# Last stage of a three-part kernel: VectorE's order written out, the weight conversions one at a time, their buffers in other places

## The chip, the cores and the metric

The kernel runs on one core of a Trainium2 chip, as one launch. The metric is the device time of one execution in microseconds (us). TensorE (PE) multiplies, VectorE (DVE), ScalarE (ACT) and GpSimd (POOL) do elementwise work, and SyncE's queue (SP) issues every DMA. Each of them takes its instructions in the order of its own list and waits at the head of that list for semaphores.

## The reference

Attention, then two two-layer networks, all in float32; only the second network matters here:

```python
def _moe2_ref(x, w_in, w_out) -> np.ndarray:
    h = x @ w_in
    relu6 = np.clip(h + 3.0, 0.0, 6.0)
    g = h * relu6 / 6.0
    return (g @ w_out).astype(np.float32)
```

There are 2304 tokens, 512 model channels and 2048 inner channels. `x` comes from the attention and the first network. The weights reach the kernel as 64-bit floats.

## The kernel before

A float32 product of full precision is built from three matmuls on rounded operands: each operand is split into a high part (`hi`, rounded by ScalarE, line 160) and a low part (`lo`, the rest, subtracted by VectorE, line 161), and hi·hi, hi·lo and lo·hi are added up in PSUM. `split` (line 158) is that pair of instructions.

The kernel runs through the attention, the first network, and then the second network in two stages. **Its first stage** (the loop at line 1008) has 32 steps. A step takes one quarter `g` of the tokens and one pair of channel blocks `j` (0 to 7) and does seven products of 6 matmuls (line 879). ScalarE holds partial sums in `z` and `m5` (line 886), VectorE adds to them (889), the gate takes one instruction of each engine (892 and 893), and the result goes to the DRAM tensor `g_scratch` (898). The products of step `j` read `w2[j]`, which lies in the buffers `wi{j}0`, `wi{j}1`, `wo{j}0` and, two steps together, `wo{j}1`. The last four steps are quarter 3 with j = 4 to 7, here called steps 28 to 31.

**Its second stage** multiplies by `w_out`. Tokens 0 to 1023 are done in two *plain blocks* of 512 tokens (`plain`, line 1042). A block takes 16 chunks `k` of 128 inner channels; a chunk has four token tiles of three matmuls of 512 columns (line 1147), 12 in all, so a block has 192. For a chunk, `gr` is loaded from `g_scratch` (1136, two chunks per load, three buffers), and split into `gh` and `gl` (three buffers each). In the second block, `make_forms` (1046) also builds from pairs of weight chunks the combinations (`tt`, then `wf2`, lines 1055 to 1063) that the remaining 1280 tokens need (line 1172, results `m`). After each block ScalarE moves the four sums to `ot` (1152), of which there are two buffers, and they are stored.

**The weights of the second stage** come in 16 chunks `k`, as 64-bit words (`wraw`, loaded by `load_out`, line 961). `to_f32` (132) turns one chunk into float32 bits: ScalarE (142), two GpSimd instructions (144, 147), two of VectorE (152, 155). The split into `wo` follows (160 on ScalarE, 161 on VectorE). `split_out` does all of it for one chunk. Chunks 0 to 7 are converted during the first stage through a spare buffer (`wcv`). Chunks 8 to 15 are called from the first plain block, one at each even `k` (line 1130), and their float32 goes to buffers `wf` that stay until `make_forms` has read them; these take the places of `w2` weights that are used no more. Which places is set by the list `slots` (950):

```python
slots = [f"{nm}{j}{i}" for j in range(4, NU) for nm in ("wi", "wo") for i in range(2)]
slots.append(slots.pop(slots.index("wo51")))
...
direct[j] = wp.tile([P, 2, CH], U32, tag=slots[NJ + j], name="wf")
```

Chunks 8 and 9 share `direct[4]`, 10 and 11 `direct[5]`, and so on; `NJ` is 8, so the four lie at slots 12 to 15: `wi71`, `wo70`, `wo71`, `wo51`.

**What sets the order.** The program is written once; a scheduler then moves instructions on each engine's list by a simulated time line, except those wrapped in `keep_in_program_order`, which keep their written order among each other. In the first plain block nothing of `split` and `to_f32` is kept; in the second, both instructions of `split(gh, gl, ...)` and VectorE's part of `make_forms` are.

Of the kernel before, what the change touches and what calls it, by code (L numbers as in the profile page):

```python
# [10 lines left out]
F32R = mybir.dt.float32r  # L11
# [4 lines left out]
P = 128  # L16
# [24 lines left out]
U32 = mybir.dt.uint32  # L41
# [20 lines left out]
def attention_moe_moe(ctx, tc, qt, kt, kq2, kqs, vs4, vp, s, w_in1, w_out1, alpha, w_in2, w_out2, out):  # L62
# [9 lines left out]
    FC = DFF // P  # L72
# [14 lines left out]
    wp = ctx.enter_context(tc.tile_pool(name="wp", bufs=1))  # L87
# [25 lines left out]
    CH = 512  # L113
# [18 lines left out]
    def to_f32(raws, pool, tag, bufs, keep, beside):  # L132

        ops = []
        for r, by in zip(raws, beside):
            c = pool.tile([P, CH], U32, tag=tag, bufs=bufs, name="wcv")
            half = r.bitcast(U16).rearrange("p f (t b) -> p f t b", t=2)
            ops.append((c, c.bitcast(F32), r[:, :, 1], r[:, :, 0], (half[:, :, 1, 0], half[:, :, 0, 1]) if by else None))

        for c, cf, high, low, by in ops:  # L140
            first = tc.keep_in_program_order if bufs == WB0 else keep
            first(nc.scalar.activation(cf, high.bitcast(F32), AF.Copy, scale=W_SCALE))  # L142
        for c, cf, high, low, by in ops:
            keep(nc.gpsimd.tensor_scalar(cf, cf, W_MOST, -W_MOST, op0=ALU.min, op1=ALU.max))  # L144

        for c, cf, high, low, by in ops:
            keep(nc.gpsimd.tensor_scalar(high.bitcast(F32), cf, 0.0, 1.0, op0=ALU.mult, op1=ALU.mult))
        for c, cf, high, low, by in ops:
            if by:
                keep(nc.scalar.activation(*by, AF.Copy, scale=1.0 / 8192, bias=-4095.5 / 8192))  # L150
        for c, cf, high, low, by in ops:
            keep(nc.vector.scalar_tensor_tensor(c, c, 3, high, op0=ALU.logical_shift_left, op1=ALU.bitwise_or))  # L152
        for c, cf, high, low, by in ops:
            if not by:
                keep(nc.vector.scalar_tensor_tensor(c, low, 29, c, op0=ALU.logical_shift_right, op1=ALU.bitwise_or))
        return [cf for c, cf, *_ in ops]

    def split(hi, lo, of, keep=lambda ins: ins):

        keep(nc.scalar.activation(hi, of, AF.Copy))  # L160
        keep(nc.vector.tensor_tensor(lo, of, hi.bitcast(F32), op=ALU.subtract))
# [589 lines left out]
    with ExitStack() as st:  # L751
        pool = Pools(st, tc, "att0", ("wcv", "vraw", "t pT"), WB0)
# [15 lines left out]
    with ExitStack() as st:  # L768
        pool = Pools(st, tc, "sb1", ("wcv g5 gh5 gl5",), WB)
        stage(s=[0], pt=[2], pv=[2], y=[1, 3, 4, 5])  # L770
        it = moe1(w1, (0, 1), pool, ("g5", "gh5", "gl5", SKEW + 1), SKEW)
        f = 0
# [34 lines left out]
    with ExitStack() as st:  # L807
        pool = Pools(st, tc, "attb", ("kraw qraw vraw ks qh vs", "t", "xf pth ptl"))
# [14 lines left out]
    NJ = FC // 2  # L823
# [28 lines left out]
    with ExitStack() as st:  # L852
        pool = Pools(st, tc, "last", ("g5 gh5 gl5 wcv",), WB)
# [94 lines left out]
    wo2, outs = {}, []  # L948
    chunks = [j + h * NJ for j in range(NJ) for h in range(2)]
    slots = [f"{nm}{j}{i}" for j in range(4, NU) for nm in ("wi", "wo") for i in range(2)]  # L950
    slots.append(slots.pop(slots.index("wo51")))
    direct = {}
# [21 lines left out]
        def tile(self, *args, **kw):  # L974
            return self.of

    def split_out(k):

        f = chunks[k]
        pool = cv  # L980
        if k >= FC // 2:
            j = f % NJ
            if j not in direct:
                direct[j] = wp.tile([P, 2, CH], U32, tag=slots[NJ + j], name="wf")
            pool = Half(direct[j][:, f // NJ])
        (cf,) = to_f32([outs[k]], pool, "wcv", 2, lambda ins: ins, (False,))
        t = wp.tile([P, 2, CH], F32R, tag=places[k][0], name="wo")
        split(t[:, 0], t[:, 1], cf)
        wo2[f] = (t[:, 0], t[:, 1])

    A1, B1 = 3, 4
    order = [(0, j) for j in range(A1)] + [(1, j) for j in range(NJ)] + [(0, j) for j in range(A1, NJ)]
# [6 lines left out]
    with ExitStack() as ph2:  # L999
# [8 lines left out]
        for i, (g, j) in enumerate(order):  # L1008
            if i in (1, 3, 5):
                with tc.high_priority(offset=WLP):  # L1010
                    w2.append(split_pair(units2[len(w2)], cv, 2))
            if i == ends[1] + 2:
                xs[2] = load_x(xb, 2)
            if i == ends[0] + 2:
                xs[3] = load_x(xa, 3)
            if i == ends[2] + 2:
                xbs.close()
                gp = late.enter_context(tc.tile_pool(name="late", bufs=2))
            if i >= ends["w", 0] + 2:
                for _ in range(2):  # L1020
                    if len(outs) < FC - 2 and i >= ends["w", places[len(outs)][1]] + 2:
                        load_out(len(outs))
                if len(wo2) < min(len(outs) - 1, FC // 2):
                    with tc.high_priority(offset=WLP):
                        split_out(len(wo2))
            step = Step(g, j, i % 2)
            if last is None:
                with tc.high_priority(offset=60):
                    for product in (step.first, step.second, step.fifth, step.sixth):
                        product()  # L1030
            else:
                for product in (step.first, last.seventh, step.second, last.third, step.sixth, step.fifth, last.fourth):
                    product()
            last = step
# [11 lines left out]
        def make_forms(j):  # L1046

            if j in direct:
                wf = direct[j].bitcast(F32)
            else:  # L1050
                wf = gp.tile([P, 2, CH], F32, tag="wf", bufs=1, name="wf")
                for h in range(2):
                    hi, lo = wo2[j + h * NJ]
                    tc.keep_in_program_order(
                        nc.vector.tensor_tensor(wf[:, h], hi.bitcast(F32), lo.bitcast(F32), op=ALU.add)
                    )
            tt = fp.tile([P, 4, ND], F32, tag="s", name="tt")
            b11, b12, b21, b22 = (wf[:, h, c * ND : (c + 1) * ND] for h in range(2) for c in range(2))
            for dst, x, y in ((0, b12, b11), (1, b22, tt[:, 0]), (2, b22, b12), (3, b21, tt[:, 1])):
                tc.keep_in_program_order(nc.vector.tensor_tensor(tt[:, dst], x, y, op=ALU.subtract))  # L1060
            t = []
            for i in range(2):
                hl = wp.tile([P, 2, 2, ND], F32R, tag=slots[2 * j + i], name="wf2")
                split(hl[:, 0], hl[:, 1], tt[:, 2 * i : 2 * i + 2])
                t += [(hl[:, 0, c], hl[:, 1, c]) for c in range(2)]
            q = [tuple(x[:, c * ND : (c + 1) * ND] for x in wo2[j + h * NJ]) for h in range(2) for c in range(2)]
            forms.append([q[0], t[2], q[2], q[3], t[0], t[1], t[3]])
# [52 lines left out]
        steps = [(t0, jp) for t0 in rest for jp in range(NJ // 2)]  # L1120
        ahead = []
        stage(o=[2, 5, 7, 0, 6, 3, 4, 1], m=[2, 5, 7, 0, 6, 3, 4, 1])
        free = lambda ins: ins
        for bi, t0 in enumerate(plain):
            ntt = NB2 // P
            op = [bank("o") for i in range(ntt)]
            for k, f in enumerate(chunks):
                if bi == 0 and k < 2:
                    load_out(len(outs))
                if bi == 0 and len(wo2) < FC and k % 2 == 0:  # L1130
                    split_out(len(wo2))
                if bi == 1 and k % 2:
                    make_forms(k // 2)
                if k % GC == 0:
                    gr = gp.tile([P, GC, NB2], F32, tag="gr", bufs=3, name="gr")
                    nc.sync.dma_start(gr, g_d.rearrange("(h j p) t -> j p h t", h=2, p=P)[f, :, :, t0 : t0 + NB2])
                gh = gp.tile([P, NB2], F32R, tag="gh", bufs=3, name="gh2")
                gl = gp.tile([P, NB2], F32R, tag="gl", bufs=3, name="gl2")
                split(gh, gl, gr[:, k % GC], tc.keep_in_program_order if bi else free)
                wh, wl = wo2[f]  # L1140
                if bi == 1 and k == FC - 4:
                    ahead.append(left_forms(*steps[0]))
                    fp.tile([P, LINE], F32, tag="line", bufs=1, name="line")
                for i in range(ntt):
                    tsl = slice(i * P, (i + 1) * P)
                    for lt, r in ((gh, wh), (gh, wl), (gl, wh)):
                        nc.tensor.matmul(  # L1147
                            op[i], lt[:, tsl], r, start=(k == 0 and r is wh and lt is gh), stop=(k == FC - 1 and lt is gl)
                        )
            for i in range(ntt):  # L1150
                ot = stg.tile([P, DM], F32, tag="yt", name="ot")
                nc.scalar.activation(ot, op[i], AF.Copy, scale=1.0 / 6.0)
                store_rows(t0 + i * P, ot)
# [61 lines left out]
```

## Time and profile before

| | us |
|---|---|
| median of three runs (1006.7, 1006.78, 1008.31) | 1006.78 |
| profiled execution, own time | 1007.25 |
| its span, first to last instruction | 1005.4 |
| PE busy | 973.0 (97%) |
| DVE busy | 696.3 (69%) |
| ACT busy | 648.3 (64%) |
| POOL busy | 449.2 (45%) |
| mean granted TensorE clock | 0.981 of full speed |

The clock is granted at full speed (1.0, 2.4 GHz) or half (0.5, 1.2 GHz); a number between is a mean over a stretch. A busy PE counts overlapping matmuls as one busy stretch, so the distance between the starts of neighbouring matmuls tells the rate. In the timeline, times are counted from the span's start.

### The profile page before, as it was taken

Reading aid. Unit: us, or ns where it says so; the run is one execution under the profiler, and the core shown is the slowest. Engines: PE = TensorE matmul, PEld = TensorE weight load, DVE = VectorE, ACT = ScalarE, POOL = GpSimd, SP = SyncE. Lnnn points to the kernel's source line nnn. Section 1 sums busy time; section 2 is a strip of 40 time slices with the busy share of each in tenths; the row PEclk is TensorE's granted clock in tenths of the full one; section 3 lists DMA queues with packets and bytes.
Section 4 is the critical chain, followed back from the end, with each engine's and each line's share of the span. In section 5 each row is a group of like instructions: output and inputs, shape, how many; then the busy total and the mean of one; then the engine's idle time right before and its main releaser. Section 6 shows DMA issues by size and latency. Waiting matters only on the chain.

```text
span 1005.4 us, 19017 instructions
## 1 busy us (share of the span) xinstructions
PE 973.0 (97%) x6578; PEld 889.9 (89%) x6578; DVE 696.3 (69%) x1655; ACT 648.3 (64%) x1442; POOL 449.2 (45%) x597
## 2 busy tenths in 40 slices
PE   7789999999999999999999999999999979999998
PEld 5568788999999998998998888999999967789998
DVE  5778884566666666666654885977658691997774
ACT  6568778678768778778754665756657652454342
POOL 5554667657666667666644763533112230000001
PEclk9779999999999999999999999999999999999999
DMA  6990014113122223122105332434258642344441
GB/s 207 303 359 3 24 30 131 40 46 91 52 76 73 59 68 97 52 70 79 52 14 185 99 104 82 166 118 147 113 189 280 238 127 84 106 146 148 126 127 42
DMA packets 64504, 114.53 MB, mean 114 GB/s; under 512 B 6280, under 2 KB 30648, under 8 KB 64408
## 3 DMA queue, kind: packets, MB, share of 16 engines
q1 hardware_dynamic: 64408, 113.32, 34.8%
q8 instruction: 52, 0.85, 0.4%
q14 instruction: 44, 0.36, 0.1%
HBM read 84.84 MB, written 28.46 MB: 113 GB/s over the span
## 4 chain that ended last, share of the span: by engine, by line
PE 88%; DVE 4%; ACT 3%; DMA 2%; issue 2%; SPq 0%; POOL 0%; ACTq 0%; DVEq 0%; POOLq 0%
PE h L248 20%; PE y L675 20%; PE m L1172 10%; PE a L879 10%; PE o L1147 7%; PE b L879 5%; PE s L410 4%; PE pv L472 4%; PE pt L447 4%; PE c L879 2%; PE pv L603 1%; PE s L322 1%; DMA wraw<-in_w_in 1%; PE pt L593 1%; DVE wf L152 1%
## 5 line engine op out<-in xcount | busy, mean ns | idle before, releaser
L248 PE MATMUL h<-xhi,wi 128*128 128x256 f32 (+1 forms) x896 | 227.6, 322 | 2.8 <-DVE gt L698 1.5
L248 PEld LDWEIGHTS h<-xhi,wi 128*128 128x128 f32 x896 | 156.7, 191 | 16.3 <-DVE gt L698 1.9
L675 PE MATMUL y<-gh,wo 128*128 128x256 f32 (+1 forms) x896 | 162.1, 315 | 0.0
L675 PEld LDWEIGHTS y<-gh,wo 128*128 128x128 f32 x896 | 133.8, 190 | 11.3 <-ACT gh L701 0.4
L248 PE MATMUL h<-xlo,wi 128*128 128x256 f32 (+1 forms) x448 | 143.4, 320 | 0.0
L879 PE MATMUL a<-x,wc 128*128 128x288 f32 x768 | 113.2, 295 | 1.1 <-ACT z L886 1.1
L879 PEld LDWEIGHTS a<-x,wc 128*128 128x128 f32 x768 | 106.0, 188 | 1.9 <-ACT z L886 1.6
L144 POOL TENSOR_SCALAR wcv<-wcv 128x512 f32<-128x512 f32 x56 | 42.0, 759 | 114.2 <-ACT wcv L142 111.2
L675 PE MATMUL y<-gl,wo 128*128 128x256 f32 (+1 forms) x448 | 91.6, 317 | 0.0
L422 POOL TENSOR_SCALAR t<-t,rec 128x384 f32<-128x384 f32 (+2 forms) x96 | 65.4, 683 | 57.5 <-DVE rec L421 32.3
L248 PEld LDWEIGHTS h<-xlo,wi 128*128 128x128 f32 x448 | 85.8, 191 | 5.9
L413 DVE CUSTOM_DVE_ANT_0 t<-s,mask 128x384 f32<-128x384 f32 (+2 forms) x96 | 53.4, 562 | 53.4 <-PE pt L447 34.1
L698 DVE SCALAR_TENSOR_TENSOR gt<-gt,beta,h 128x256 f32<-128x256 f32 (+1 forms) x112 | 61.6, 552 | 30.7 <-ACT gt L697 29.5
L1147 PE MATMUL o<-wo,gh 128*128 128x512 f32 x256 | 74.6, 406 | 7.9 <-ACT wo L160 4.2
L1112 POOL TENSOR_TENSOR ot<-u,e 128x256 f32<-128x256 f32 x5 | 3.9, 783 | 171.5 <-DVE u L1106 153.9
L418 ACT ACTIVATE t<-t,m 128x384 f32<-128x384 f32 (+2 forms) x96 | 67.1, 700 | 17.0 <-DVE m L413 15.8
L675 PEld LDWEIGHTS y<-gl,wo 128*128 128x128 f32 x448 | 69.7, 190 | 6.0 <-issue 0.2
L702 POOL TENSOR_TENSOR gl<-gt,gh 128x256 fp32r<-128x256 f32 x80 | 59.1, 740 | 30.2 <-ACT gh L701 28.3
L701 ACT ACTIVATE gh<-gt 128x256 fp32r<-128x256 f32 (+1 forms) x112 | 53.1, 477 | 29.7 <-DVE gt L698 28.1
L383 POOL TENSOR_TENSOR ks<-kraw,ks 64x576 fp32r<-64x576 f32 (+1 forms) x40 | 52.4, 1311 | 41.1 <-issue 33.6
L1147 PEld LDWEIGHTS o<-wo,gh 128*128 128x128 f32 x256 | 50.0, 197 | 20.2 <-ACT wo L160 4.7
L697 ACT ACTIVATE gt<-h 128x256 f32<-128x256 f32 (+1 forms) x112 | 48.7, 439 | 20.8 <-PE h L248 14.4
(172 smaller groups left out, 2390.2 us busy)
## 6 DMA issues: line engine op xcount, KB each, us to landing
g_scratch<-gt SPq DMA_DIRECT2D x64, 288.0 KB
wraw<-in_w_in SPq DMA_DIRECT2D x32, 512.0 KB
wraw<-in_w_out SPq DMA_DIRECT2D x32, 512.0 KB
gq<-g_scratch SPq DMA_DIRECT2D x40, 256.0 KB
kraw<-in_kt SPq DMA_DIRECT2D x32, 288.0 KB
gr<-g_scratch SPq DMA_DIRECT2D x16, 512.0 KB
qraw<-in_qt SPq DMA_DIRECT2D x32, 160.0 KB
vraw<-in_vp SPq DMA_DIRECT2D x32, 160.0 KB
```

The source lines that it names most:

```text
L248: nc.tensor.matmul(dst, lt, r, start=first and i == 0, stop=last and i == len(terms) - 1)
L383: nc.gpsimd.tensor_tensor(ks[D:P], kraw[D:P], ks[D:P].bitcast(F32), op=ALU.subtract)
L413: nc.vector.tensor_tensor_reduce(t[:n, a:e], sc[:n, : e - a], mask[:n, MASK + n - (e - a) :][:, : e - a] if e == w else mask[:n, : e - a], ...
L418: nc.scalar.activation(t[:n, :w], t[:n, :w], AF.Exp, bias=m[-1][:n], scale=-1.0, accum_out=den[:n])
L422: nc.gpsimd.tensor_scalar(t[:n, :w], t[:n, :w], rec[:n], 1.0, op0=ALU.mult, op1=ALU.mult)
L675: nc.tensor.matmul(ys[dc // per][:, o : o + n], which[:, dc * P : (dc + 1) * P], gg, start=(f == 0 and which is wl and dc % per == 0), sto ...
L698: nc.vector.scalar_tensor_tensor(gt, gt, beta[:, f : f + 1], hp[:, :n], op0=ALU.mult, op1=ALU.add)
L701: nc.scalar.activation(gh, gt, AF.Copy)
L702: (nc.vector if n == 512 else nc.gpsimd).tensor_tensor(gl, gt, gh.bitcast(F32), op=ALU.subtract)
L879: nc.tensor.matmul(dst[:, :NX2], lt, r, start=first and n == 0, stop=n == len(terms) - 1, skip_group_check=not first,)
L1147: nc.tensor.matmul(op[i], lt[:, tsl], r, start=(k == 0 and r is wh and lt is gh), stop=(k == FC - 1 and lt is gl))
L1172: nc.tensor.matmul(acc[i], lt, r, start=(j == 0 and x == 0 and k % 2 == 0), stop=(j == NJ - 1 and x == 2 and (k % 2 == 1 or k == 6)),)
```

## The change

There are four parts. The buffers of `direct` move from slots 12 to 15 to slots 0 to 3 (`wi40`, `wi41`, `wo40`, `wo41`), and those of `wf2` move four slots on. `split_out` is cut in two, `out_f32` (to float32) and `split_out` (into hi and lo), and the first plain block calls the one at odd and the other at even `k`, one chunk at a time, behind the `split` of that chunk. VectorE's instructions of these, from k = 3 on and in the whole second block, keep their written order (`in_order`); ScalarE's are left to the scheduler in both blocks. `make_forms` is called behind the `split` of its chunk.

```diff
+    def in_order(ins):
+        return tc.keep_in_program_order(ins) if ins.ins.engine == mybir.EngineType.DVE else ins
+
+    def out_f32(k, keep=free):
...
-                direct[j] = wp.tile([P, 2, CH], U32, tag=slots[NJ + j], name="wf")
+                direct[j] = wp.tile([P, 2, CH], U32, tag=slots[j - NJ // 2], name="wf")
             pool = Half(direct[j][:, f // NJ])
-        (cf,) = to_f32([outs[k]], pool, "wcv", 2, lambda ins: ins, (False,))
+        return to_f32([outs[k]], pool, "wcv", 2, keep, (False,))
+
+    def split_out(k, cf, keep=free):
+
         t = wp.tile([P, 2, CH], F32R, tag=places[k][0], name="wo")
-        split(t[:, 0], t[:, 1], cf)
-        wo2[f] = (t[:, 0], t[:, 1])
+        split(t[:, 0], t[:, 1], cf[0], keep)
+        wo2[chunks[k]] = (t[:, 0], t[:, 1])
...
-                        split_out(len(wo2))
+                        split_out(len(wo2), out_f32(len(wo2)))
...
-                hl = wp.tile([P, 2, 2, ND], F32R, tag=slots[2 * j + i], name="wf2")
+                hl = wp.tile([P, 2, 2, ND], F32R, tag=slots[(NJ // 2 + 2 * j + i) % len(slots)], name="wf2")
...
-                if bi == 0 and len(wo2) < FC and k % 2 == 0:
-                    split_out(len(wo2))
-                if bi == 1 and k % 2:
-                    make_forms(k // 2)
+                hold = in_order if bi or k > 2 else free
+                if bi == 0 and k == 0:
+                    split_out(FC // 2, out_f32(FC // 2))
...
-                split(gh, gl, gr[:, k % GC], tc.keep_in_program_order if bi else free)
+                split(gh, gl, gr[:, k % GC], hold)
+                if bi == 0 and k and k % 2 == 0:
+                    split_out(FC // 2 + k // 2, cf, hold)
+                if bi == 0 and k % 2 and k < FC - 1:
+                    cf = out_f32(FC // 2 + k // 2 + 1, hold)
+                if bi == 1 and k % 2:
+                    make_forms(k // 2)
```

All five engines' lists are unchanged up to the last steps of the first stage. Three places differ most.

VectorE's list where chunk 8 is converted. `wf_10914` is the float32 of chunks 8 and 9, `wo_10920` the split weights of chunk 8; `gl2_11098` belongs to chunk 8 of the first plain block. Before:

```order
L152 SCALAR_TENSOR_TENSOR wf_11086<-wf_11086,wraw_10603 128x512
L161 TENSOR_TENSOR gl2_11098<-gr_11095,gh2_11097 128x512
L155 SCALAR_TENSOR_TENSOR wf_11086<-wraw_10603,wf_11086 128x512
L152 SCALAR_TENSOR_TENSOR wf_10914<-wf_10914,wraw_10453 128x512
L161 TENSOR_TENSOR gl2_11114<-gr_11095,gh2_11113 128x512
L161 TENSOR_TENSOR wo_11134<-wf_11086,wo_11134 128x512
L152 SCALAR_TENSOR_TENSOR wf_10914<-wf_10914,wraw_10455 128x512
L155 SCALAR_TENSOR_TENSOR wf_10914<-wraw_10453,wf_10914 128x512
L152 SCALAR_TENSOR_TENSOR wf_11171<-wf_11171,wraw_10912 128x512
L155 SCALAR_TENSOR_TENSOR wf_10914<-wraw_10455,wf_10914 128x512
L161 TENSOR_TENSOR gl2_11140<-gr_11137,gh2_11139 128x512
```

Now, with `gl2_10986` belonging to chunk 3 of the block and `gt`, `z` and `m5` to the last steps of the first stage:

```order
L893 SCALAR_TENSOR_TENSOR gt_10765<-gt_10765,a_10687 128x288
L152 SCALAR_TENSOR_TENSOR wf_10914<-wf_10914,wraw_10453 128x512
L155 SCALAR_TENSOR_TENSOR wf_10914<-wraw_10453,wf_10914 128x512
L161 TENSOR_TENSOR wo_10920<-wf_10914,wo_10920 128x512
L889 TENSOR_TENSOR m5_8672<-a_10749,m5_8672 128x288
L889 TENSOR_TENSOR z_10812<-c_10830,z_10812 128x288
L889 TENSOR_TENSOR z_10750<-b_10794,z_10750 128x288
L893 SCALAR_TENSOR_TENSOR gt_10827<-gt_10827,m5_8672 128x288
L152 SCALAR_TENSOR_TENSOR wf_10914<-wf_10914,wraw_10455 128x512
L893 SCALAR_TENSOR_TENSOR gt_10845<-gt_10845,z_10750 128x576
L155 SCALAR_TENSOR_TENSOR wf_10914<-wraw_10455,wf_10914 128x512
L161 TENSOR_TENSOR wo_10970<-wf_10914,wo_10970 128x512
```

Chunk 8, which stood behind the conversions of chunks 10 to 13 and 15 and beside the `gl` of its own use, now stands first of the eight, ahead of the `gl` of chunk 3.

ScalarE's list at steps 28 and 29 (`gt_10703` and `z_10614` are of step 28, `z_10688` of step 29). Before:

```order
L892 ACTIVATE gt_10629<-a_10539,three_78 128x288
L886 ACTIVATE z_10688<-a_10687 128x288
L892 ACTIVATE gt_10703<-m5_8672,three_78 128x288
L892 ACTIVATE gt_10721<-z_10614,three_78 128x576
L160 ACTIVATE gh2_10925<-gr_10923 128x512
L160 ACTIVATE gh2_10943<-gr_10923 128x512
L886 ACTIVATE z_10688<-a_10687 128x288
```

Now, `wraw_10601` and `wraw_10603` being chunks 12 and 13, the last two that are loaded before the `gr`:

```order
L892 ACTIVATE gt_10629<-a_10539,three_78 128x288
L142 ACTIVATE wf_11074<-wraw_10601 128x512
L886 ACTIVATE z_10688<-a_10687 128x288
L142 ACTIVATE wf_10914<-wraw_10453 128x512
L142 ACTIVATE wf_10914<-wraw_10455 128x512
L142 ACTIVATE wf_11074<-wraw_10603 128x512
L892 ACTIVATE gt_10703<-m5_8672,three_78 128x288
L892 ACTIVATE gt_10721<-z_10614,three_78 128x576
L160 ACTIVATE gh2_10925<-gr_10923 128x512
L160 ACTIVATE gh2_10943<-gr_10923 128x512
L886 ACTIVATE z_10688<-a_10687 128x288
```

Four conversions that stood beside and behind step 31 are now between steps 28 and 29; two more (chunks 10 and 11) follow ahead of step 30's first `z`.

ScalarE's list between the two plain blocks: `gh2_11240` is chunk 15 of the first, the next two `gh2` are chunks 0 and 1 of the second. Before:

```order
L160 ACTIVATE gh2_11240<-gr_11222 128x512
L1152 ACTIVATE ot_11256<-o_10908 128x512
L1152 ACTIVATE ot_11259<-o_10909 128x512
L1152 ACTIVATE ot_11262<-o_10910 128x512
L1152 ACTIVATE ot_11265<-o_10911 128x512
L160 ACTIVATE gh2_11274<-gr_11272 128x512
```

Now:

```order
L160 ACTIVATE gh2_11240<-gr_11219 128x512
L160 ACTIVATE gh2_11274<-gr_11272 128x512
L160 ACTIVATE gh2_11290<-gr_11272 128x512
L1165 ACTIVATE ot_11256<-o_10908 128x512
L1165 ACTIVATE ot_11259<-o_10909 128x512
L160 ACTIVATE gh2_11322<-gr_11320 128x512
L160 ACTIVATE wf2_11302<-tt_11297 128x512
L160 ACTIVATE wf2_11305<-tt_11297 128x512
L1165 ACTIVATE ot_11262<-o_10910 128x512
L160 ACTIVATE gh2_11338<-gr_11320 128x512
```

The first two `gh` of the second block moved ahead of all four `ot`, and the last two `ot` behind them.

## Rows read from the trace of the kernel before

**Rows 1.** The page's first part: TensorE's busy time, share, instructions.

```profile
PE 973.0 (97%) x6578; PEld 889.9 (89%) x6578; DVE 696.3 (69%) x1655; ACT 648.3 (64%) x1442; POOL 449.2 (45%) x597
```

**Rows 2.** Windows: length, busy us per engine (instructions), granted clock, DMA share, GB/s.

```profile
786.00:795.50 9.50, 8.65 (x65) 8.42 (x64) 8.37 (x17) 7.29 (x16) 0.00 (x0) 1.00 0.75 258
...
822.50:826.70 4.20, 0.01 (x1) 0.00 (x0) 4.20 (x8) 1.78 (x3) 0.00 (x0) 1.00 0.52 163
826.70:835.00 8.30, 7.42 (x19) 5.38 (x20) 4.18 (x7) 1.89 (x3) 0.00 (x0) 0.59 0.07 20
...
855.20:860.00 4.80, 4.55 (x13) 3.37 (x14) 4.70 (x10) 2.00 (x5) 0.00 (x0) 0.68 0.24 86
860.00:900.00 40.00, 40.00 (x177) 33.13 (x178) 38.85 (x76) 19.65 (x32) 0.00 (x0) 1.00 0.38 113
```

**Rows 3.** Timeline of TensorE: start, us, instruction, [idle before, releaser].

```profile
822.12 0.39 PE L1147 MATMUL o<-wo,gl 128*128 128x512 f32 x1
826.75 1.46 PE L1147 MATMUL o<-wo,gh 128*128 128x512 f32 x4 [4.23 <-ACT wo L160]
...
851.12 0.62 PE L1147 MATMUL o<-wo,gh 128*128 128x512 f32 x2
...
851.80 0.62 PE L1147 MATMUL o<-wo,gh 128*128 128x512 f32 x2
852.25 0.39 PE L1147 MATMUL o<-wo,gl 128*128 128x512 f32 x1
855.26 3.48 PE L1147 MATMUL o<-wo,gh 128*128 128x512 f32 x8 [2.62 <-ACT gh L160]
...
859.84 2.11 PE L1147 MATMUL o<-wo,gh 128*128 128x512 f32 x8 [0.19 <-ACT gh L160]
...
900.77 0.52 PE L1172 MATMUL m<-wo,ga 128*128 128x256 f32 x3
```

**Rows 4.** Timeline of ScalarE at the two holes.

```profile
826.06 0.63 ACT L160 ACTIVATE wo<-wf 128x512 fp32r<-128x512 f32 x1 [1.86 <-DVE wf L155]
...
850.64 1.28 ACT L1152 ACTIVATE ot<-o 128x512 f32<-128x512 f32 x2 [5.71 <-PE o L1147]
853.42 1.27 ACT L1152 ACTIVATE ot<-o 128x512 f32<-128x512 f32 x2 [1.51 <-DMA out<-ot]
854.59 0.62 ACT L160 ACTIVATE gh<-gr 128x512 fp32r<-128x512 f32 x1
```

**Rows 5.** The chain of waits: the first `gr` load. Columns: start, us, what.

```profile
780.44 5.63 DMA gr<-g_scratch
```

**Rows 6.** Timeline of SyncE's queue: the loads of chunks 12 and 13.

```profile
776.75 0.94 SPq L965 DMA_DIRECT2D wraw<-in_w_out  x2
```

**Rows 7.** Timeline of ScalarE, steps 28 to 30 of the first stage.

```profile
780.65 0.49 ACT L892 ACTIVATE gt<-a,three 128x288 f32<-128x288 f32 x1
...
786.10 1.15 ACT L160 ACTIVATE gh<-gr 128x512 fp32r<-128x512 f32 x2 [1.23 <-DMA gr<-g_scratch]
787.15 0.39 ACT L886 ACTIVATE z<-a 128x288 f32<-128x288 f32 x1
...
789.35 0.40 ACT L886 ACTIVATE z<-a 128x288 f32<-128x288 f32 x1
```

**Rows 8.** Timeline of TensorE: step 29's seventh, step 30's sixth, three products up to step 30's seventh.

```profile
787.60 1.07 PE L879 MATMUL a<-x,wc 128*128 128x288 f32 x6 [0.84 <-ACT z L886]
...
790.09 0.96 PE L879 MATMUL a<-x,wc 128*128 128x288 f32 x6
...
791.68 2.56 PE L879 MATMUL a<-x,wc 128*128 128x288 f32 x18
```

**Rows 9.** Timeline of VectorE: the gate that frees a PSUM bank.

```profile
793.22 0.45 DVE L893 SCALAR_TENSOR_TENSOR gt<-gt,a 128x288 f32<-128x288 f32 x1 [0.41 <-ACT gt L892]
```

**Rows 10.** Tile `wf` from 770 to 860: count, ns min/median/max, first and last start, form.

```profile
L142 ACT ACTIVATE wf<-wraw x8: 656/669/681, 799.0 to 814.6; 128x512 f32<-128x512 f32 x8
...
L152 DVE SCALAR_TENSOR_TENSOR wf<-wf,wraw x8: 685/890/1120, 807.2 to 825.9; 128x512 uint32<-128x512 uint32 x8
```

More of the change, by code (lines that the diff above doesn't have):

```diff
@@ L975, in tile, with free @@
             return self.of
-    def split_out(k):
+    def free(ins):
+        return ins
+    def in_order(ins):
+        return tc.keep_in_program_order(ins) if ins.ins.engine == mybir.EngineType.DVE else ins
+    def out_f32(k, keep=free):
         f = chunks[k]
@@ L1122, in attention_moe_moe @@
         stage(o=[2, 5, 7, 0, 6, 3, 4, 1], m=[2, 5, 7, 0, 6, 3, 4, 1])
-        free = lambda ins: ins
         for bi, t0 in enumerate(plain):
```

## The prediction

> **What bounds the kernel now.** I read the page first: TensorE is busy 97% of the span, and no other engine over 70% [rows 1]. So only a change that shortens TensorE's idle time or its slow clock moves the end. The lists are the same up to the last steps of the first stage, at about 781 us; I read everything from there to the end of the second plain block. The windows there [rows 2] show where TensorE isn't full: a little in 786 to 795.5 (8.65 of 9.50 us), nothing in 822.5 to 826.7, a mean clock of 0.59 behind that, and 0.68 in 855.2 to 860. The mean of 0.59 is a mix of half speed (1.2 GHz) and full speed. From 860 to 900 TensorE is full at clock 1.00. So two holes, each with a stretch of half clock behind it.
>
> TensorE's own timeline gives their places [rows 3]. The first stands before the 97th matmul of the first plain block (96 have started by 822.12), that is at chunk 8: TensorE waits 4.23 us for ScalarE's `wo`. ScalarE's timeline has that instruction at 826.06, itself late because VectorE's line 155 was [rows 4]. VectorE was busy for all of 4.20 us in that window [rows 2]: it was working through conversions of later chunks, as its list shows, since chunks 8 and 9 go to `wi71`, a weight buffer of the last step, and are converted behind those of 10 to 13 and 15. The second hole stands between the blocks: 2.62 us until `gh` of the second block's chunk 0, which ScalarE does at 854.59, behind four `ot`, two of which wait for the store of the first two [rows 4]. From 860 on VectorE is busy 38.85 of 40 us [rows 2], which matters for what could go wrong.
>
> **What the two holes cost.** At full clock three matmuls start in 851.80 − 851.12 = 0.68 us, so one in 0.227 [rows 3]. Chunk 8 would have started at 822.12 + 0.23 = 822.35, and 96 matmuls later, at 844.1, the block would have been over. It was over at 852.25 + 0.23 = 852.48. First hole with its clock: 8.4 us. From 852.48 to the first `m` at 900.77 are 48.3 us; 192 matmuls need 43.5. Second hole with its clock and a wait of 0.19 [rows 3]: 4.8 us. Together 13.1 (13.2 by the rounded terms).
>
> **What the change does to them.** The new places `wi40` to `wo41` are freed by step 28, not 31. Chunk 8 becomes the first conversion on VectorE, ahead of `gl` of chunk 3, five chunks or 5 × 12 × 0.227 = 13.6 us ahead of its use; each later one is written four chunks ahead of its use, with one conversion (three instructions of VectorE, 0.69 each alone [rows 10]) and two `gl` of the same size for every two chunks: 5 × 0.69 = 3.45 us of VectorE in 5.44 us of TensorE. So I take the first hole as gone. At the second, `gh` of chunks 0 and 1 stand before the `ot`, and their buffers are free when TensorE has done chunks 13 and 14. The two `ot` that wait for stores now stand behind `gh` of chunks 2 and 3. The store took until 853.42 from 851.92, when its `ot` pair ended [rows 4], and chunk 3 starts 3 × 2.72 = 8.2 us into the block, so they have room. I take the second hole as gone too. The moved `wf2` places and the later `make_forms` cost nothing by themselves: same instructions, and `gl` of two chunks now goes ahead of the eight form instructions behind them. If that cover goes, a pair of chunks has only the 1.15 us in 40 in which VectorE was idle, 0.16 us a pair.
>
> **What the change adds.** No instruction is added: 16 conversions as before. But six of ScalarE's (line 142, 0.67 us each [rows 10], about 0.57 when two follow on each other, like the two `gh` in 1.15 [rows 7]) now stand inside the first stage, in front of instructions that TensorE waits for. The first converts chunk 12, whose load was issued at 776.75 with that of chunk 13 [rows 6]. No row shows these landing; the nearest is `gr`, 5.63 us from issue [rows 5], in the same queue: chunk 12 at about 776.75 + 0.47 + 5.63 = 782.9. Bounds: under 780.65 + 0.49 = 781.1 it costs no wait at all, and not after 786.1, when the `gr` behind it had landed [rows 7]. I take 782.9. ScalarE, free at 781.1, waits there until 782.9; queued behind it are step 29's `z`, step 28's gates and both first `gh`, and TensorE and VectorE wait for these. Then 0.57 + 0.35 for the `z` (783.8), three more conversions (785.5), two gates of 0.45 and 0.67 (786.7), two `gh` (787.8), and the next `z` ends at 788.2. Before, TensorE went on at 787.60, directly behind that `z` [rows 7, 8]: 0.6 late. Then `m5`, a `gh`, a `wo`, a gate, the two conversions of chunks 10 and 11 and the `z` of step 30: 0.3 + 0.57 + 0.57 + 0.4 + 1.14 + 0.35 = 3.35, so 791.55, where the sixth product of step 30 started at 790.09 [rows 8]: 1.4 late in all. Then ten of the block's matmuls have been put in between the twelfth and the last six of the 18 that started at 791.68 [rows 8], so at 791.68 + 12 × 0.133 = 793.3, now 794.7. They write a bank that VectorE's gate frees, at 793.67 before [rows 9]; that gate is late by ScalarE's 1.4 and by about 0.5 for what the new list puts ahead of it on VectorE, 795.6: another 0.9.
>
> VectorE is full there, so its own instructions count. Line 152 took 0.685 us alone and up to 1.12 [rows 10]. What makes the difference is in that row's window GpSimd's conversions, which now fall among the gates: three such instructions of VectorE at 0.43 more would add 1.3, none 0; nothing in the rows decides, and I take 0.7. By the Trainium skill ("GPSIMD Engine Reference", section 8, Key points) GpSimd shares its SBUF interfaces with VectorE, and VectorE's instructions with two SBUF inputs suffer; that speaks against moving conversions beside the gates, and by it the 1.3 would be due in full, 0.6 more than I take: 997.3 for the median. The spread of line 152 is in line with it.
>
> Sum of what is added: 1.4 + 0.9 + 0.7 = 3.0. Its bounds: below, −0.8, if the loads land early and even the old wait of 0.84 [rows 8] goes; above, 1.4 + 0.9 + 1.3 = 3.6, and the clock. TensorE would now stand idle about 1 to 2 us at a time. Behind 0.84 us of idle the clock stayed at 1.00, behind 2.62 and 4.23 it fell [rows 2, 3]. A fall costs what is left of the holes without their delays: 8.4 − (826.75 − 822.35) − 0.83 (a second wait, for `lo`) = 3.1 to 3.2, or 4.8 − (855.26 − 852.48) − 0.19 = 1.8. So up to 6.8.
>
> **The sum.** The profiled execution took 1007.25: 1007.25 − 13.1 + 3.0 = 997.15. It stood 0.47 above the median of 1006.78, so 996.7 for the median. Own range of this case: 993 to 998.
>
> **Rivals.**
> 1. *The clock falls in the first stage.* One of the new waits is long enough, or chunk 12 lands later than 782.9 (every 1 us of lateness is 1 us at ScalarE's head). For it: DMA share 0.75 in that window [rows 2]. Against: ScalarE is busy only 7.29 of 9.50 us there, and each wait is nearer to 0.84 than to 2.62. 996.7 + 1.8 to 3.2: about 999.5.
> 2. *The second hole is only exchanged.* The fourth load of `gr` for the second block stands in SyncE's list ahead of the four stores, and it waits for `gl` of that block's chunk 1; ScalarE's third `ot` waits for a store and stands ahead of `gh` of chunk 3. If that ring closes late, TensorE stops at chunk 3 instead of chunk 0: 996.7 + 4.8 = 1001.5. Against: `gl` of chunk 1 can be done when TensorE is still in chunk 15.
> 3. *The first hole stays in part.* The change doesn't do what it says: ScalarE still begins with chunk 12, not 8, and chunk 14 is loaded last, behind a `gr` that waits for `gl` of chunk 5. If that stops ScalarE so long that a `gh` is late, half of the first hole is back: 996.7 + 4.2 = 1000.9.
> 4. *Slower.* In the second block VectorE has 0.16 us to spare for each pair of chunks. ScalarE now does `gh` of a chunk still waiting for TensorE ahead of the two `wf2` that VectorE waits for. If ScalarE's part of a pair is exposed on VectorE, TensorE follows it: four conversions of 0.6 are 2.4, less 0.16, over 8 pairs 17.9 us: 1014. It decides from (10.1 / 8) + 0.16 = 1.4 us of exposure for a pair. For it: VectorE at 97% there [rows 2]. Against: `gl` now comes two chunks before its use, and VectorE, which waited for the `gh` of 854.59 [rows 4], enters the block ahead.
>
> **How the numbers follow.** Forecast 0.70, rivals 0.12, 0.08, 0.04 and 0.06. About 0.2% (2 us) is what a measurement of this kernel can tell from no change. All but the fourth are faster by more: 0.93, with 0.01 of the fourth near zero for "same", and 0.06 slower; I give 0.92, 0.02, 0.06. The range of 8 in 10: from 993.4 (added cost about nothing) to 1001.6, the second rival; what lies outside is the fourth and the forecast's lowest end.
>
> **What the new profile would show.** Right: no wait of TensorE over 1 us between the first stage's end and the first `m`; `wo` of chunk 8 converted before `gl` of chunk 3; clock 1.00 from 800 to 900; the first plain block over near 852.5 − 8.4 + 3.0 = 847, the first `m` near 891. The added cost: ScalarE idle before line 142 of chunk 12, ended by the load, and TensorE waits for `z` at steps 29 and 30 and for VectorE before the first matmuls of the block. Wrong: a clock under 1.00 in 783 to 800; waits for `gl` at even chunks of the second block; TensorE full in the first stage's end, which would make the 3.0 too large.

## The result and the profile after

| | median us | ratio to before, 95% interval |
|---|---|---|
| before, runs beside the first comparison | 1006.74 | |
| changed kernel, first comparison | 996.01 | 0.9892 [0.9867, 0.9918] |
| changed kernel, second comparison | 997.17 | 0.9919 [0.9897, 0.9941] |
| changed kernel, third comparison | 994.59 | 0.9896 [0.9878, 0.9913] |

The change makes the kernel about 1% faster, 8 to 11 us. The first profiled execution of the changed kernel took 1177.08 us at a mean granted clock of 0.748; it is left out of the table (with it the first median is 997.08) and of the ratios, and all rows below are of another one, which took 993.83 us (span 991.7).

The times of one kernel spread by several us (the kernel before: 1004.39 to 1010.13 in one comparison of 12 runs), so I also measure inside the traces, from one landmark to another: from SyncE's load of chunks 12 and 13 [rows 6] to the first `m` product [rows 3]. From the first `m` to the span's end it was 104.6 us in each of these traces; the load's own time varied, over all traces below, from 774.35 to 780.01.

| trace | load, us | first `m`, us | stretch, us |
|---|---|---|---|
| before [rows 3, 6] | 776.75 | 900.77 | 124.02 |
| before, again | 780.01 | 903.66 | 123.65 |
| changed | 775.91 | 887.10 | 111.19 |
| changed, again | 776.64 | 888.48 | 111.84 |

So the stretch is 11.8 to 12.8 us shorter, where the prediction had 13.1 − 3.0 = 10.1. The changed kernel's page begins with this line (as [rows 1]):

```profile
PE 968.5 (98%) x6578; PEld 888.4 (90%) x6578; DVE 694.0 (70%) x1655; ACT 648.0 (65%) x1442; POOL 449.0 (45%) x597
```

The same windows view as [rows 2] (length, busy us of PE, PEld, DVE, ACT, POOL, granted clock, DMA share, GB/s):

```profile
783.00:795.50 12.50, 11.56 (x78) 10.70 (x78) 12.50 (x20) 8.67 (x19) 8.83 (x10) 1.00 0.67 225
820.00:830.00 10.00, 10.00 (x46) 8.28 (x45) 8.55 (x14) 3.98 (x7) 0.00 (x0) 1.00 0.54 159
840.00:850.00 10.00, 10.00 (x46) 8.29 (x45) 6.99 (x13) 5.97 (x10) 0.00 (x0) 1.00 0.48 146
...
860.00:887.00 27.00, 27.00 (x121) 22.38 (x120) 25.50 (x52) 14.63 (x24) 0.00 (x0) 1.00 0.39 118
```

Where the kernel before had its two holes TensorE is full, and the clock is 1.00. TensorE's timeline, all rows with a wait from 778 to 905, and the first `m` (as [rows 3, 8]):

```profile
788.60 1.06 PE L879 MATMUL a<-x,wc 128*128 128x288 f32 x6 [0.30 <-ACT z L886]
791.88 1.06 PE L879 MATMUL a<-x,wc 128*128 128x288 f32 x6 [0.64 <-DVE gt L893]
...
887.10 0.52 PE L1185 MATMUL m<-wo,ga 128*128 128x256 f32 x3
```

Two waits are left, both in the first stage, 0.94 us together: one for `z`, one for VectorE's gate. 192 matmuls at 0.227 are 43.6 us, so the first plain block was over near 887.10 − 43.6 = 843.5.

### The profile page after: what moved, and what is told of

Same layout as the page of the kernel before. It is cut to its first block, busy times and chain, and to the rows that moved or that the text cites. A ratio compares the mean times of both kernels' runs of the same rounds, so it can differ in the third digit from the quotient of the medians.

```text
span 1175.0 us, 19011 instructions
## 1 busy us (share of the span) xinstructions
PE 1155.3 (98%) x6578; PEld 1016.9 (87%) x6578; DVE 686.7 (58%) x1655; ACT 653.3 (56%) x1442; POOL 437.8 (37%) x597
## 4 chain that ended last, share of the span: by engine, by line
PE 95%; DMA 2%; ACT 1%; issue 1%; DVE 1%; POOL 0%; SPq 0%; DVEq 0%; POOLq 0%; ACTq 0%
PE h L248 21%; PE y L675 20%; PE a L879 10%; PE m L1185 10%; PE o L1160 9%; PE b L879 5%; PE s L410 5%; PE pv L472 4%; PE pt L447 4%; PE c L879 3%; PE s L322 2%; DMA vraw<-in_vs 1%; PE h L534 1%; DMA kr<-cum_scratch 1%; PE pv L603 1%
## 5 line engine op out<-in xcount | busy, mean ns | idle before, releaser
L248 PE MATMUL h<-xhi,wi 128*128 128x256 f32 (+1 forms) x896 | 264.5, 363 | 0.7 <-ACT xhi L611 0.5
L248 PEld LDWEIGHTS h<-xhi,wi 128*128 128x128 f32 x896 | 174.3, 211 | 25.3 <-ACT xhi L611 0.9
L675 PE MATMUL y<-gh,wo 128*128 128x256 f32 (+1 forms) x896 | 193.0, 358 | 0.0
L675 PEld LDWEIGHTS y<-gh,wo 128*128 128x128 f32 x896 | 151.4, 211 | 22.9
L248 PE MATMUL h<-xlo,wi 128*128 128x256 f32 (+1 forms) x448 | 162.1, 362 | 0.2 <-DVE xlo L612 0.2
L879 PE MATMUL a<-x,wc 128*128 128x288 f32 x768 | 134.1, 331 | 0.0
L879 PEld LDWEIGHTS a<-x,wc 128*128 128x128 f32 x768 | 125.5, 201 | 0.8
L675 PE MATMUL y<-gl,wo 128*128 128x256 f32 (+1 forms) x448 | 107.3, 359 | 0.0
L879 PE MATMUL b<-x,wc 128*128 128x288 f32 x384 | 72.3, 332 | 0.0
L452 ACT ACTIVATE pth<-pt 128x384 fp32r<-128x384 f32 (+2 forms) x96 | 46.9, 488 | 43.3 <-PE pt L447 21.8
```

The lines of the kernel that those rows point to most:

```text
L248: nc.tensor.matmul(dst, lt, r, start=first and i == 0, stop=last and i == len(terms) - 1)
L675: nc.tensor.matmul(ys[dc // per][:, o : o + n], which[:, dc * P : (dc + 1) * P], gg, start=(f == 0 and which is wl and dc % per == 0), sto ...
L879: nc.tensor.matmul(dst[:, :NX2], lt, r, start=first and n == 0, stop=n == len(terms) - 1, skip_group_check=not first,)
```

## The experiments

All are compared with runs of the kernel before on the same chip.

**The changed kernel again.** No edit.

> The changed kernel once more, for its own trace. Theory (both holes gone, about 3 us added at the end of the first stage): 996 us (993 to 998); between the end of the first stage and the first m product no wait of TensorE over 1 us and a granted clock of 1.00; the first plain block over near 847, the first m near 891; ScalarE idle before line 142 of chunk 12, ended by that chunk's load, and TensorE waits for z at steps 29 and 30. Rival 1 (the clock falls in the first stage): a clock under 1.00 in 783 to 800 and the first m 2 to 3 us later, 999. Rival 2 (part of the first hole stays at another chunk): a wait of 1 to 4 us for wo or gl in the first block, which would then be over near 849 to 851.

Measured: 997.17 us, ratio 0.9919 [0.9897, 0.9941], and the rows above. Both holes are gone, and no rival came; but the block was over 843.5 − 775.91 = 67.6 us after the load and not 847 − 776.75 = 70.2, so most of the 3.0 that the prediction added isn't there. ScalarE's timeline at the early conversions (line 142 of tile `wf`; as [rows 7]):

```profile
779.79 0.50 ACT L892 ACTIVATE gt<-a,three 128x288 f32<-128x288 f32 x1
780.19 0.68 ACT L142 ACTIVATE wf<-wraw 128x512 f32<-128x512 f32 x1
780.77 0.39 ACT L886 ACTIVATE z<-a 128x288 f32<-128x288 f32 x1
781.16 1.81 ACT L142 ACTIVATE wf<-wraw 128x512 f32<-128x512 f32 x3
782.88 0.52 ACT L892 ACTIVATE gt<-m,three 128x288 f32<-128x288 f32 x1
783.30 0.76 ACT L892 ACTIVATE gt<-z,three 128x576 f32<-128x576 f32 x1
783.97 1.14 ACT L160 ACTIVATE gh<-gr 128x512 fp32r<-128x512 f32 x2
785.01 0.39 ACT L886 ACTIVATE z<-a 128x288 f32<-128x288 f32 x1
```

No row has a bracket: ScalarE waits for nothing here. The load of chunk 12, issued at 775.91, had landed by 780.19, at most 4.28 us later.

**The kernel before again.** No edit.

> The kernel before once more, for a second trace of it, since the traces differ by more (12.8 us from the load of chunks 12 and 13 to the first m product) than the times do (8 to 11). Theory (the stretch from that load to the first m is fixed by the order of the lists): 124.0 us again within 0.5, both holes at the same places (waits of 4.2 and 2.6 us), and whatever else differs lies ahead of 776 us; time 1003 to 1008. Rival (the holes are of random size): a stretch of 120 to 123 us and a first hole of another size.

Measured: 1006.34 us, ratio 1.0008 [0.9994, 1.0022]; stretch 123.65. TensorE's timeline at the two holes:

```profile
830.08 2.07 PE L1147 MATMUL o<-wo,gh 128*128 128x512 f32 x4 [4.22 <-ACT wo L160]
...
858.12 2.12 PE L1147 MATMUL o<-wo,gh 128*128 128x512 f32 x8 [2.62 <-ACT gh L160]
```

The two waits are as in [rows 3], so the two holes are not a matter of chance; the smaller waits behind them do vary (0.21 and 1.54 here, where the first trace had 0.83 and 0.19). ScalarE's timeline of the same trace, at steps 28 and 29:

```profile
785.84 0.54 ACT L892 ACTIVATE gt<-m,three 128x288 f32<-128x288 f32 x1 [0.96 <-DVE m L889]
787.36 0.78 ACT L892 ACTIVATE gt<-z,three 128x576 f32<-128x576 f32 x1 [0.98 <-DVE z L889]
789.44 1.15 ACT L160 ACTIVATE gh<-gr 128x512 fp32r<-128x512 f32 x2 [1.31 <-DMA gr<-g_scratch]
```

So in the kernel before ScalarE was idle ahead of these three instructions, for 0.96 + 0.98 + 1.31 = 3.25 us in all. In the changed kernel the early conversions stand there, and no row has a bracket.

**The changed kernel a third time.** No edit.

> The changed kernel once more. Theory (a stretch fixed by the lists, and a load of chunks 12 and 13 that lands 4 to 5 us after its issue, earlier than the 6.15 that the prediction took): from that load to the first m product 111.2 us within 0.7, TensorE's waits there under 1 us; the rest of a difference to the 993.8 us of the first trace lies ahead of that load. Rival (the load lands later in some executions, and then the 2 to 3 us of the prediction are due): 113 to 114 us, ScalarE idle for 1 us or more before line 142 of chunk 12.

Measured: 994.59 us, ratio 0.9896 [0.9878, 0.9913], stretch 111.84, TensorE's waits 0.18, 0.49 and 0.46. This time ScalarE did wait for the load, 5.02 us after its issue at 776.64. ScalarE's row, and TensorE's for step 30's sixth product:

```profile
781.66 0.67 ACT L142 ACTIVATE wf<-wraw 128x512 f32<-128x512 f32 x1 [0.63 <-DMA wraw<-in_w_out]
...
789.96 1.06 PE L879 MATMUL a<-x,wc 128*128 128x288 f32 x6 [0.49 <-ACT z L886]
```

So the predicted wait exists, at 0.63 and not at the predicted 1.8. This stretch is 0.65 longer than the other's.

**Only the places.** The kernel before, with the two new slot expressions alone:

```diff
-                direct[j] = wp.tile([P, 2, CH], U32, tag=slots[NJ + j], name="wf")
+                direct[j] = wp.tile([P, 2, CH], U32, tag=slots[j - NJ // 2], name="wf")
...
-                hl = wp.tile([P, 2, 2, ND], F32R, tag=slots[2 * j + i], name="wf2")
+                hl = wp.tile([P, 2, 2, ND], F32R, tag=slots[(NJ // 2 + 2 * j + i) % len(slots)], name="wf2")
```

> The kernel before, with only the new places of the converted weights; the order in which the work is written is the old one. Theory (the first hole is the place of chunk 8 alone; the second is ScalarE's order): the first hole of 8.4 us goes, the second of 4.8 stays, the early conversions cost their 3.0 as in the changed kernel: 1006.7 - 8.4 + 3.0 = 1001.3; no wait of TensorE for wo of chunk 8, but 2 to 3 us for gh between the blocks with a clock under 1.00 behind it. Rival (VectorE needs the written order too): VectorE converts chunks 12, 8, 13, 9 and 10 ahead of gl of chunk 3, so TensorE waits 2 us or more for that gl, and the time is 1004 to 1008.

Measured: 1000.43 us, ratio 0.9950 [0.9931, 0.9969], stretch 893.23 − 776.82 = 116.41. All waits of TensorE in it:

```profile
790.12 1.05 PE L879 MATMUL a<-x,wc 128*128 128x288 f32 x6 [0.50 <-ACT z L886]
793.23 1.06 PE L879 MATMUL a<-x,wc 128*128 128x288 f32 x6 [0.46 <-DVE gt L893]
847.73 3.60 PE L1147 MATMUL o<-wo,gh 128*128 128x512 f32 x8 [2.62 <-ACT gh L160]
```

The first hole is gone with the places alone, without a written order for VectorE: given the early places, the scheduler itself moves the conversions forward, and VectorE's first line 152 of a `wf` starts at 796.11, where it was 807.16 before. The second hole stands as it was. The rival's wait for `gl` of chunk 3 did not come.

**Only the order.** The changed kernel with the old slot expressions, the edit above the other way round.

> The changed kernel with the old places of the converted weights: chunks 8 and 9 lie in a buffer of the last step again, and VectorE's written order has their six instructions ahead of gl of chunk 3. Theory (without the places the first hole is exchanged, not closed): those six come behind the last gate of the first stage, 4.1 to 6 us in all, while TensorE has come to chunk 3; a wait of TensorE of 3 to 6 us for gl of chunk 3, with a clock under 1.00 behind it; the second hole is gone: about 1006.7 - 4.8 and 0 to 3 us either way, 1000 to 1003. Rival (the written order alone closes both holes, and without the early conversions nothing is added): 992 to 994, no wait over 1 us.

Measured: 1005.22 us, ratio 1.0001 [0.9983, 1.0019], stretch 897.65 − 774.83 = 122.82. The theory's place was right and its size wrong: a wait of 3 to 6 us and a time of 1000 to 1003 were expected, and the wait is 10.12. TensorE's timeline at chunk 3:

```profile
806.14 1.55 PE L1160 MATMUL o<-wo,gh 128*128 128x512 f32 x6
817.81 2.07 PE L1160 MATMUL o<-wo,gl 128*128 128x512 f32 x4 [10.12 <-DVE gl L161]
```

VectorE's timeline ahead of that `gl`:

```profile
812.38 2.13 DVE L152 SCALAR_TENSOR_TENSOR wf<-wf,wraw 128x512 uint32<-128x512 uint32 x2 [5.05 <-POOL wraw L147]
814.43 1.28 DVE L155 SCALAR_TENSOR_TENSOR wf<-wraw,wf 128x512 uint32<-128x512 uint32 x2
815.86 1.29 DVE L161 TENSOR_TENSOR wo<-wf,wo 128x512 fp32r<-128x512 f32 x2 [0.15 <-ACT wo L160]
817.08 0.68 DVE L161 TENSOR_TENSOR gl<-gr,gh 128x512 fp32r<-128x512 f32 x1
```

GpSimd's timeline, the instructions for which VectorE waits:

```profile
811.01 0.61 POOL L144 TENSOR_SCALAR wf<-wf 128x512 f32<-128x512 f32 x1 [1.63 <-ACT wf L142]
811.71 2.27 POOL L147 TENSOR_SCALAR wraw<-wf 128x512 f32<-128x512 f32 x3
```

ScalarE's instruction for which GpSimd waits:

```profile
810.27 0.66 ACT L142 ACTIVATE wf<-wraw 128x512 f32<-128x512 f32 x1 [2.33 <-DMA wraw<-in_w_out]
```

And the windows behind the wait (columns as above):

```profile
817.80:826.00 8.20, 8.19 (x24) 6.52 (x25) 7.22 (x12) 2.53 (x4) 0.00 (x0) 0.65 0.43 128
826.00:897.00 71.00, 71.00 (x315) 58.77 (x314) 54.81 (x103) 31.98 (x53) 0.00 (x0) 1.00 0.40 119
```

`gl` of chunk 3 stands behind the six instructions of chunks 8 and 9, as expected. What I had left out is that the first of them waits 5.05 us for GpSimd, whose last three (line 147) stand behind a conversion for which GpSimd in turn waits until ScalarE has done line 142 of another chunk; and ScalarE starts that one at 810.27, when the chunk's load has landed. So a written order without the places puts conversions that come late at VectorE's head, where the whole block waits for them: 10.1 and the clock in exchange for both old holes. How much of the 10.1 is the place, and how much that load, this run does not separate.

**ScalarE kept in order in the second block.**

```diff
-                hold = in_order if bi or k > 2 else free
+                hold = tc.keep_in_program_order if bi else in_order if k > 2 else free
```

> The changed kernel, with ScalarE's instructions too kept in the written order in the second block: its four ot stand ahead of gh of chunk 0 again. Theory (the second hole is ScalarE's order alone): the hole is back, 2 to 3 us of wait for gh between the blocks and a clock under 1.00 behind it: the changed kernel's time + 4.8, about 1000.7. Rival (the hole was closed by what VectorE does earlier): within 1 us of the changed kernel, no wait over 1 us there.

Measured: 999.5 us, ratio 0.9935 [0.9911, 0.9958], stretch 894.88 − 779.16 = 115.72. ScalarE's timeline between the blocks:

```profile
845.00 1.28 ACT L1165 ACTIVATE ot<-o 128x512 f32<-128x512 f32 x2 [5.65 <-PE o L1160]
847.77 1.28 ACT L1165 ACTIVATE ot<-o 128x512 f32<-128x512 f32 x2 [1.49 <-DMA out<-ot]
848.95 1.14 ACT L160 ACTIVATE gh<-gr 128x512 fp32r<-128x512 f32 x2
```

And TensorE's row behind it:

```profile
849.62 3.21 PE L1160 MATMUL o<-wo,gh 128*128 128x512 f32 x8 [2.62 <-ACT gh L160]
```

The second hole is back to the hundredth, with the same four `ot` and the same wait for a store as [rows 4]. It is ScalarE's order alone.

**ScalarE kept in order in the first block, twice.** Four of the six early conversions go behind the first stage:

```diff
-                hold = in_order if bi or k > 2 else free
+                hold = in_order if bi else tc.keep_in_program_order if k > 2 else free
```

> The changed kernel, with ScalarE's instructions in the written order from chunk 3 of the first block on: four of the six early conversions (line 142 of chunks 10 to 13) stand behind the first stage; chunks 8 and 9 are still converted early. Theory (the early conversions on ScalarE cost the 3.0 us added in the first stage, most of it by the wait for chunk 12's load and by four instructions more): 1.5 to 2.5 us faster than the changed kernel, about 994; no idle time of ScalarE ended by the load of chunk 12, and z of steps 29 and 30 as early as in the kernel before. Rival (what is added comes from elsewhere, VectorE or the memory): within 0.5 us of the changed kernel. Second rival (ScalarE's conversions now between the gh of the block make a gh late): slower than the changed kernel by 1 us or more, with waits for gh in the first block.

> The changed kernel with ScalarE's instructions in the written order from chunk 3 of the first block on, once more beside the two others. Theory: from the load of chunks 12 and 13 to the first m product 110.0 us within 0.5, no wait of TensorE in it, 1 to 1.5 us less than the changed kernel; time 0.1 to 0.3% under it. Rival (the gain of the first comparison was chance): the same time as the changed kernel within 0.1%, and a stretch within 0.5 us of its.

Measured: 994.02 us, ratio 0.9886 [0.9868, 0.9905], stretch 887.77 − 777.80 = 109.97; again 993.33 us, 0.9886 [0.9867, 0.9906], 886.26 − 775.68 = 110.58. The window of the first of these traces at the first stage's end, as [rows 2] (there TensorE had 8.65 of 9.50):

```profile
783.00:795.50 12.50, 12.50 (x90) 12.00 (x89) 11.90 (x22) 8.72 (x19) 4.26 (x5) 1.00 0.79 262
```

TensorE has no wait at all in the first trace, and 0.60 for `z` in the second, behind a late `gr`. Both stretches are 1.2 to 1.3 us under the changed kernel's of the same comparison. That is less than the 1.5 to 2.5 us that were expected first. The times agree in sign (3.2 and 1.3 us under it in the medians), but their intervals overlap with its; that this version is faster than the changed one is shown by the traces, not by the times alone. It has the shortest stretch of the kernels run.

**The forms early.** `make_forms` of the second block back ahead of `gh` and `gl`:

```diff
+                if bi == 1 and k % 2:
+                    make_forms(k // 2)
                 if k % GC == 0:
                     gr = gp.tile([P, GC, NB2], F32, tag="gr", bufs=3, name="gr")
...
-                if bi == 1 and k % 2:
-                    make_forms(k // 2)
```

> The changed kernel, with make_forms of the second block back ahead of gh and gl of the odd chunks. Theory (that move costs and brings nothing, since VectorE enters the block ahead): from the load of chunks 12 and 13 to the first m product 111.5 us within 0.7, as in the changed kernel, no wait of TensorE over 1 us in the second block, time 994 to 997. Rival (the eight form instructions, 4.4 us of VectorE by 2 x 0.69 + 4 x 0.42 + 2 x 0.69, make gl of chunk 1 late): a wait of 1 to 3 us for gl of chunk 1 with a clock under 1.00 behind it, 113 to 116 us, time 997 to 1001.

Measured: 994.64 us, ratio 0.9894 [0.9870, 0.9918], stretch 886.22 − 774.35 = 111.87, no wait of TensorE behind the first stage, and two for `z` in it (0.44 and 0.80). Here the load of chunk 12 landed 5.27 us after its issue:

```profile
779.62 0.68 ACT L142 ACTIVATE wf<-wraw 128x512 f32<-128x512 f32 x1 [0.89 <-DMA wraw<-in_w_out]
```

That part of the change brings nothing and costs nothing, as the prediction had it.

## Why the prediction was right, and where its sum was not

**The first hole (8.4): right, and its cause.** The places alone take 124.02 or 123.65 to 116.41, 7.2 to 7.6, about the 8.4 less what is added. The written order alone takes 0.8 to 1.2 off and has a larger hole. VectorE's written order, which the prediction counted on, is not needed to close the first hole; the late buffer was the cause, as the prediction said, since with the early one the scheduler puts the first conversions ahead by itself.

**The second hole (4.8): right.** Put back, it costs 115.72 − 111.19 or − 111.84: 4.5 or 3.9. With the places alone, where it was never taken away, 116.41 stands 4.6 to 5.2 over the changed kernel.

**What is added (3.0): the step that failed, by its size.** 124.02 − 13.1 = 110.9 is the stretch without holes; the changed kernel has 111.2 and 111.8, so 0.3 to 0.9 were added, in the lower half of the bounds that the prediction gave (−0.8 to 3.6). By its terms:
- *1.4 for `z` behind early conversions: the landing time was wrong, the chain behind it right.* The term rested on a load that lands 6.15 us after issue, taken from a `gr`; it landed after at most 4.28, after 5.02, and after 5.27 with the forms early, so ScalarE waited 0 to 0.89 us and not 1.8. From line 142 of chunk 12 to the first `gh` it then took 783.97 − 780.19 = 3.78 us, where the prediction had 786.7 − 782.9 = 3.8: the four conversions went into the time in which ScalarE had been idle, as the prediction's chain had it. ScalarE came to this `gh` 783.97 − 775.91 = 8.06 and 785.34 − 776.64 = 8.70 us after the load's issue; before, `gr` had let it start after 786.10 − 776.75 = 9.35 [rows 6, 7]. And `gr` was early in both traces, for ScalarE did not wait for it. So step 30's sixth product, which was to be 1.4 late, started 788.60 − 775.91 = 12.69 and 789.96 − 776.64 = 13.32 us after that issue, against 790.09 − 776.75 = 13.34 before [rows 8]: not late at all. That is in part luck: with a `gr` as late as before, it would have been late by 12.69 + (9.35 − 8.06) − 13.34 = 0.64, an estimate from these rows.
- *0.9 for the bank that VectorE's gate frees: there, smaller, and in another place.* TensorE waits 0.64 and 0.46 for a gate in the two traces of the changed kernel, but before a product of line 879. The gate is the one at 791.38 below, one step ahead of that of [rows 9], and the block's first matmuls, for which the prediction had the wait, follow without one.
- *0.7 for VectorE beside GpSimd.* VectorE lost more than I took, and TensorE less. VectorE's timeline in the changed kernel, in the first of the two traces:

```profile
783.74 0.86 DVE L893 SCALAR_TENSOR_TENSOR gt<-gt,m 128x288 f32<-128x288 f32 x1
784.52 1.09 DVE L155 SCALAR_TENSOR_TENSOR wcv<-wraw,wcv 128x512 uint32<-128x512 uint32 x1
785.54 1.20 DVE L893 SCALAR_TENSOR_TENSOR gt<-gt,z 128x576 f32<-128x576 f32 x1
786.66 2.74 DVE L161 TENSOR_TENSOR gl<-gr,gh 128x512 fp32r<-128x512 f32 x3
789.32 0.45 DVE L889 TENSOR_TENSOR m<-a,m 128x288 f32<-128x288 f32 x1
...
791.38 0.44 DVE L893 SCALAR_TENSOR_TENSOR gt<-gt,a 128x288 f32<-128x288 f32 x1
...
792.48 0.68 DVE L155 SCALAR_TENSOR_TENSOR wcv<-wraw,wcv 128x512 uint32<-128x512 uint32 x1
793.08 0.45 DVE L893 SCALAR_TENSOR_TENSOR gt<-gt,m 128x288 f32<-128x288 f32 x1
793.45 0.74 DVE L893 SCALAR_TENSOR_TENSOR gt<-gt,z 128x576 f32<-128x576 f32 x1
```

And GpSimd's in the same stretch:

```profile
783.37 1.70 POOL L144 TENSOR_SCALAR wf<-wf 128x512 f32<-128x512 f32 x2
785.15 2.10 POOL L147 TENSOR_SCALAR wraw<-wf 128x512 f32<-128x512 f32 x2
787.77 2.10 POOL L144 TENSOR_SCALAR wf<-wf 128x512 f32<-128x512 f32 x2 [0.51 <-ACT wf L142]
789.95 2.63 POOL L147 TENSOR_SCALAR wraw<-wf 128x512 f32<-128x512 f32 x3
```

The first three rows against the last three are the same forms, first with GpSimd busy and then with GpSimd done (its last ends at 789.95 + 2.63 = 792.58): 0.86, 1.09, 1.20 against 0.45, 0.68, 0.74, 1.28 more in three instructions, just the 0.43 each that the prediction took. The three `gl` behind them are longer too. `m<-a,m` and `gt<-gt,a`, which have an input in PSUM, are not. Nor did every instruction with two inputs in SBUF lengthen: line 152 at 783.13 took 0.68 and `wo<-wcv,wo` at 789.69 took 0.73, both with GpSimd busy. TensorE's only wait for VectorE there is 0.64, the bank's. The prediction had counted 0.9 for the bank and 0.7 for this, one on top of the other: they are one wait. By the Trainium skill ("GPSIMD Engine Reference", section 8, Key points) GpSimd's SBUF interfaces are shared with VectorE, which shows in VectorE's instructions with two SBUF inputs. The trace agrees in the lengthened rows and in the two with an input in PSUM; by that rule the term would have been 1.3, and further off.

**The rivals.** The clock stayed at 1.00 in 783 to 795.5, behind waits of 0.30 and 0.64. The store that rival 2 spoke of does hold ScalarE, ahead of `gh` of chunk 3, and this `gh` is still early enough (no wait of TensorE there):

```profile
847.15 0.60 ACT L1165 ACTIVATE ot<-o 128x512 f32<-128x512 f32 x1 [1.62 <-DMA out<-ot]
847.65 0.62 ACT L160 ACTIVATE gh<-gr 128x512 fp32r<-128x512 f32 x1
```

Rival 3's late load of chunk 14 holds ScalarE too, for 4.09 us, and costs TensorE nothing:

```profile
817.23 0.66 ACT L142 ACTIVATE wf<-wraw 128x512 f32<-128x512 f32 x1 [4.09 <-DMA wraw<-in_w_out]
```

For rival 4, VectorE is busy 25.50 of 27.00 us in the second block, and TensorE waits for it nowhere.

**The number.** 996.7 was forecast; 996.01, 997.17 and 994.59 were measured. By the traces alone it should have come out 1.7 to 2.7 us lower, since the stretch lost 11.8 to 12.8 and not 10.1. The ratios give 8 to 11. So the number came out closer than its sum: 2 us or more too much was taken for what is added, and something else of about that size made up for it. That is luck. What lies between must be ahead of the load of chunks 12 and 13, where the two kernels' lists are the same and the traces of one kernel already differ by 3.3 us, or in executions of which there is no trace; the runs don't settle it.

## What to carry to other kernels

Find the place that the late data lies in before you write an order: with an early buffer the scheduler's own order closed the hole, and with a late buffer the written order gave a wait of 10.12 us for one of 4.23. When you put instructions ahead of others on an engine, look at the brackets of the rows behind them: idle time there takes them first. A landing time taken from another load's row is a guess; carry its spread through the sum, for here most of a term hung on it. And where times spread by more than the effect, compare the distance between two landmarks that stand in both lists.

## What the runs showed of the hardware

- What a hole costs in clock is not in proportion to the wait. By the window's length times what is missing to a clock of 1.00, an estimate, a wait of 2.62 cost 1.5 us more (4.80 × 0.32), one of 4.23 cost 3.4 more (8.30 × 0.41, with a second wait of 0.83 in the window) [rows 2], and one of 10.12 cost 2.9 more (8.20 × 0.35).
- The same load on the same queue landed within 4.28 us of its issue in one execution, and after 5.02 and 5.27 in others; a `gr` after 5.63 [rows 5], and within 783.97 − 779.60 = 4.37 in the changed kernel.
